# A GpSimd cast order, a per-head DMA transpose call and a planner rule in a fused attention and MLP kernel

## The chip, the cores and the metric

The kernel runs on one core of a Trainium2 chip. The metric is the device time of one execution in microseconds (us), the median of several runs. The engines named below are PE (TensorE, the matrix unit), DVE (VectorE), ACT (ScalarE), POOL (GpSimd) and SP (SyncE, which here only issues transfers). Each engine has its own instruction stream and works it off in order; 16 DMA engines move data for all of them.

## The reference

Eight batches, eight heads, 576 positions, head dimension 64. The first four heads ("plain") attend to the last 32 positions, the last four ("dilated") to every fourth of the last 128. The result, as 4608 rows of 512, goes through an MLP with 2048 hidden columns and a gated activation; its output is 4608 x 512 in float32.

```python
    window = 32
    dilation = 4
    scale = 1.0 / np.sqrt(D)
    scores = scale * np.matmul(q, k.transpose(0, 1, 3, 2))
...
    rel = pos[:, None] - pos[None, :]
    mask_plain = (rel >= 0) & (rel < window)
    mask_dil = (rel >= 0) & (rel < window * dilation) & (rel % dilation == 0)
...
    attn = attn / (np.sum(attn, axis=-1, keepdims=True) + 1e-09)
    return np.matmul(attn, v).astype(np.float32)
...
    h = x @ w_in
    g = h * (1.0 / (1.0 + np.exp(-beta * h)))
    return (g @ w_out).astype(np.float32)
```

## The kernel before

All inputs are float32, and the matmuls run in bfloat16. The 4608 token rows are cut into nine tiles of 512. Tile `t` needs the attention output `xT` of the batches that its rows lie in (a batch has 576 rows), then 16 groups of four matmuls with `w_in` (L887, one group for each 128 columns of the hidden layer), tanh on ACT (L896), the gate on DVE (L901), and four blocks of 16 matmuls with `w_out` (L922), whose sums ACT or DVE scale into one of four `osb` buffers (L937, L939) and SP stores (L942). The attention of batch `b` is worked in between the matmuls of tile `b - 1`.

The order on every engine is written down ahead of time. The program describes each step as an `Op` with the engines that may do it, a duration, dependencies and a due number `vt`; `Plan.run` (L64) plays the steps against its own model of engines, PSUM banks and DMA queues and emits them in the order that it finds. `NUDGE` (L47) shifts single steps by step number. Where PE would be idle in the model's first 80 us it emits a filler matmul on zeros (L1035).

Keys and queries reach PE with the head dimension on the partitions. For batches 0 to 2 they are loaded by position and turned on PE (L469, L479). For batches 3 to 7 (`b >= DIRECT`) each of four groups (`z` 0 keys, 1 queries; `h0` 4 the dilated heads, 0 the plain ones) takes two DMA steps:

- `cast` (L443): POOL issues a DMA from the float32 input to a bfloat16 scratch tensor in DRAM. Dilated groups are copied in the input's own order, as 16 x 9 runs of 1024 elements. Plain groups are copied into the order position, head, element, so in 2304 runs of 64 elements.
- `crossbar` (L453): SP issues one `dma_start_transpose` of the scratch tensor, viewed as 576 rows of 256 columns, into SBUF tiles of 128 partitions x 2 x 576: `dk` and `dq` for the dilated heads, `kT` and `qT` for the plain ones.

`loads(b)` (L985) starts them: POOL's one-element copy `pace` (L1001) waits until both halves of `xT` of batch `b - 2` and all four transposes of batch `b - 1` have landed; then come the casts, the value loads and, on SP, the transposes. The plain scores of a batch of this kind are 24 matmuls in one step, named `S00` (L711), which needs both `kT` and `qT`. The attention's result leaves through DRAM: SP stores `xsp`, `xdm` and `xdt` (L506, L514, L519) and turns them into `xT` (L533).

Of the kernel before, what the change touches and what calls it, by code (L numbers as in the profile page):

```python
# [39 lines left out]
class Plan:  # L40
# [3 lines left out]

    CAPS = {"h": 3, "p": 4, "o": 2, "z": 4, "a": 8, "s": 5, "w": 6}
    SWITCH = 95
    NUDGE = {9: -400, 35: 400, 78: -150, 90: 150, 103: -900, 156: -900, 164: -60, 191: -60, 208: 150,  # L47
        220: 900, 247: -400, 251: 60, 266: -150, 268: -150, 270: -150, 326: 900, 376: 400,
        397: 900, 420: 900, 432: -900, 490: 900, 525: 150, 545: 60, 554: 900, 562: -60, 571: 60,
        574: 150, 1103: -400, 1113: 400}  # L50
    LAT = {"PE": 210, "ACT": 45, "DVE": 45, "POOL": 60, "SP": 0}
    NEAR = {"PE": 40, "ACT": 60, "DVE": 60, "POOL": 60, "SP": 0}

# [10 lines left out]
    def run(self, filler=None, filler_until=0.0):  # L64
        free = {"PE": 1100.0, "ACT": 1300.0, "DVE": 1000.0, "POOL": 1300.0, "SP": 1300.0}
        dma_free = {"POOL": 0.0, "SP": 0.0, "ACT": 0.0}
        lanes = {"POOL": [], "SP": [], "ACT": []}
        bank_free = {b: 0.0 for b in self.banks}
        held = {}
        for o in self.ops:  # L70
            for d in o.deps:
                d.next.append(o)
            o.waits = len(o.deps)
            o.ready = 0.0
        avail = [o for o in self.ops if not o.waits]
        n_left = len(self.ops)
        n_held = {k: 0 for k in self.CAPS}
        ends = []
        halves = False
        port = {"DVE": 0.0, "POOL": 0.0}  # L80

        def release(now):
            for g in list(ends):
                if g.release <= now:
                    ends.remove(g)
                    n_held[g.kind] -= 1

        def bank_at(gs, start):
            kind, more = gs[0].kind, len(gs)
            n = [x.release for x in ends if x.kind == kind and x.release > start]  # L90
            n_open = sum(1 for x in held.values() if x.kind == kind)
            if n_open + more > self.CAPS[kind]:
                return None
            over = n_open + len(n) - self.CAPS[kind] + more
            if over > 0:
                start = sorted(n)[over - 1]
            open_banks = {x.bank for x in held.values()}
            times = sorted(t for b, t in bank_free.items() if b not in open_banks)
            return max(start, times[more - 1]) if len(times) >= more else None

        while n_left:
            best = None
            near = {}
            for o in avail:
                base = o.ready
                at = {e: max([free[e], base] + [t for x, t in o.group.read.items() if x != e]
                             if o.group is not None and e != "PE" else [free[e], base]) for e, d in o.engs}
                if o.sbuf:
                    at = {e: max(t, port["DVE" if e == "POOL" else "POOL"]) for e, t in at.items()}
                fin = min(at[e] + d for e, d in o.engs)  # L110
                for e, d in o.engs:
                    start = at[e]
                    if start + d > fin + 100:
                        continue
                    if o.dma and len(lanes[e]) >= 8:
                        start = max(start, lanes[e][-8])
                    if o.acquire is not None:
                        start = bank_at(o.acquire, start)
                        if start is None:
                            continue  # L120
                    near.setdefault(e, []).append((start, o, d))
            picks = []
            for e, c in near.items():
                first = min(s + o.bias for s, o, _ in c)
                s, o, d = min((x for x in c if x[0] + x[1].bias <= first + self.NEAR[e]), key=lambda x: (x[1].vt, x[0]))
                picks.append((s, o.vt, e, o, d))
            assert picks, "no work can start"
            s, _, e, o, d = min(picks, key=lambda x: (x[0], x[1]))
            if filler is not None and s <= filler_until and free["PE"] + (300 if free["PE"] < COLD else 170) < s:
                now = free["PE"]  # L130
                open_banks = {x.bank for x in held.values()}
                spare = [b for b, t in bank_free.items() if b not in open_banks and t <= now]
                if spare:
                    filler(max(spare, key=lambda b: -bank_free[b]))
                free["PE"] = now + (225 if now < COLD else 115)
                halves = False
                continue
            for g in o.acquire or ():
                open_banks = {x.bank for x in held.values()}
                g.bank = min((b for b, t in bank_free.items() if b not in open_banks and t <= s + 1e-6),  # L140
                             key=lambda b: -bank_free[b])
                held[id(g)] = g
                g.left = len(g.users)
            o.fn(e)
            if e == "PE" and o.halves != halves:
                halves = o.halves
                d += self.SWITCH
            free[e] = s + d
            if o.sbuf:
                port[e] = s + d  # L150
            o.start, o.end = s, s + d + self.LAT[e]
            if o.group is not None and e != "PE":
                o.group.read[e] = o.end
            if o.dma:
                at = max(dma_free[e], s + d + 900)
                other = max(dma_free.values()) - at
                dma_free[e] = at + o.dma + max(0.0, min(o.dma, other))
                o.end = dma_free[e] + (o.lat or 1100)
                lanes[e].append(o.end)
            avail.remove(o)  # L160
            n_left -= 1
            for x in o.next:
                x.waits -= 1
                x.ready = max(x.ready, o.end)
                if not x.waits:
                    avail.append(x)
            for g in list(held.values()):
                if o in g.users:
                    g.left -= 1
                    if not g.left:  # L170
                        del held[id(g)]
                        g.release = max(u.end for u in g.users)
                        bank_free[g.bank] = g.release
                        ends.append(g)
            ends[:] = [g for g in ends if g.release > s - 5000]
        self.end = max(free.values())
# [8 lines left out]
def kernel(  # L185
# [10 lines left out]
    nc = tc.nc  # L196
    P = 128
    B, H, S, D = q.shape
# [5 lines left out]
    WIN = 32  # L204
    C = 4
# [29 lines left out]
    plan = Plan(range(8))  # L235
# [47 lines left out]
    kT = [const([P, 2, WIN + S], BF16, f"kT{i}") for i in range(2)]  # L283
    qT = [const([P, 2, S], BF16, f"qT{i}") for i in range(2)]
    qt = [const([P, 2, 2, 4, UT], BF16, f"qt{i}") for i in range(2)]
    dk = [const([P, 2, 4, CT], BF16, f"dk{i}") for i in range(2)]
# [109 lines left out]
    def load(queue, args, deps, vt, kb, rate=.4, issue=750, lat=1100):  # L396
        return plan.op(
            [(queue, issue)],
            lambda e: dma(queue, *args), deps, vt, dma=kb * 1024 / rate / 1000, lat=lat)
# [41 lines left out]
    scratch = {}  # L441

    def cast(b, z, h0, deps, vt):  # L443

        dst = scratch[b, z, h0] = dram_pool.tile([S * 4 * D], BF16, name=f"s{b}_{z}_{h0}")
        src = (k, q)[z][b, h0:h0 + 4]
        if h0:
            args = [x.rearrange("(a c e) -> c a e", c=16, e=1024) for x in (dst[:], src.rearrange("h s d -> (h s d)"))]
        else:
            args = (dst[:].rearrange("(s h d) -> s h d", h=4, d=D), src.rearrange("h s d -> s h d"))  # L450
        return load("POOL", args, deps, vt, 576, .38 if h0 else .2, 500 if h0 else 1700)

    def crossbar(b, z, h0, deps, vt):  # L453
        kv = b % 2
        if h0:
            dst = (dk, dq)[z][kv][:].rearrange("p r h t -> p r (h t)")
        else:
            dst = qT[kv][:] if z else kT[kv][:, :, WIN:]
        src = scratch[b, z, h0][:].rearrange("(a e) -> a e", e=C * D)
        return plan.op([("SP", 1300)], lambda e: nc.sync.dma_start_transpose(out=dst, in_=src),  # L460
                       deps, vt, dma=288 * 1024 / .2 / 1000, lat=5500 if b == DIRECT else 6500)


# [605 lines left out]
```

## Time and profile before

| | us |
|---|---|
| median of 3 runs | 303.01 (302.78 to 303.18) |
| the profiled execution | 302.73 |
| its span in the trace | 301.0 |
| PE busy | 295.5 (98%) |
| DVE busy | 187.5 (62%) |
| ACT busy | 172.2 (57%) |
| POOL busy | 83.9 (28%) |
| plain transposes (L460): first `kT` issue, last `qT` issue | 67.0, 192.8 |
| plain scores `S00` of batches 3 to 7 (L711): first, last | 85.7, 215.2 to 215.7 |

The span runs from the first to the last instruction that the trace shows; the 1.7 us to the profiled execution's own time lie around it. An engine's busy time leaves out the issuing of DMAs, so SP has none; its instructions are listed as SPq, and their durations are those of the issue, not of the transfer.

### The profile page before, as it was taken

How to read it: one execution, taken by the hardware profiler on the slowest of the kernel's cores; microseconds unless marked ns; L12 is line 12 of the kernel's file. 1: busy time of each engine (PE TensorE's matmuls, PEld its weight loads, DVE VectorE, ACT ScalarE, POOL GpSimd, SP SyncE). 2: the span in 40 equal slices, each digit the busy share in tenths (PEclk: the TensorE clock that was granted, in tenths of full speed). 3: DMA queues.
4: the chain of work that ended last, by engine and by line, in shares of the span. 5: the costliest groups of instructions: out<-in, count | busy, mean ns of one | idle time of the engine just before them, and what ended most of it. 6: DMA issues, size and time to landing. Idle time of an engine off the chain costs nothing.

```text
span 301.0 us, 6071 instructions
## 1 busy us (share of the span) xinstructions
PE 295.5 (98%) x2344; PEld 150.4 (50%) x2344; DVE 187.5 (62%) x424; ACT 172.2 (57%) x311; POOL 83.9 (28%) x121
## 2 busy tenths in 40 slices
PE   8999999999999999999999999999999999999995
PEld 5866546444554445544444544444454444444454
DVE  4769787798857846887677647865772363343300
ACT  3868764867745744667484548454852654554311
POOL 8997324764236006400730074000000000000000
PEclk9999999999999999999999999999999999999999
DMA  8999999899889998999899979993124100100122
GB/s 164 188 210 201 206 178 222 122 133 145 196 188 197 158 199 173 199 158 191 145 172 158 224 146 173 179 211 90 37 74 117 70 1 35 37 35 35 59 82 70
DMA packets 111248, 41.98 MB, mean 139 GB/s; under 512 B 87620, under 2 KB 104596, under 8 KB 111220
## 3 DMA queue, kind: packets, MB, share of 16 engines
q0 software_dynamic: 60336, 18.58, 59.5%
q1 hardware_dynamic: 50740, 22.95, 37.8%
q8 instruction: 18, 0.29, 0.4%
q14 instruction: 10, 0.08, 0.1%
q10 hardware_dynamic: 144, 0.07, 0.1%
HBM read 37.76 MB, written 18.87 MB: 188 GB/s over the span
## 4 chain that ended last, share of the span: by engine, by line
PE 94%; DVE 2%; ACT 1%; POOL 1%; issue 1%; POOLq 0%; ACTq 0%
PE bank L922 41%; PE bank L887 40%; PE bank L804 2%; PE bank L1035 2%; PE bank L683 1%; PE bank L788 1%; PE bank L711 1%; PE bank L469 1%; PE bank L747 1%; PE bank L479 1%; ACT ptd L619 1%; PE bank L773 1%; DVE xdm L639 1%; PE bank L673 1%; DVE ptd L623 1%
## 5 line engine op out<-in xcount | busy, mean ns | idle before, releaser
L922 PE MATMUL bank<-w_out_bf,g 128*128 128x512 bf16 (+2 forms) x608 | 140.0, 368 | 0.0
L901 DVE SCALAR_TENSOR_TENSOR g<-tnh,bank 128x512 bf16<-128x512 bf16 x144 | 97.3, 685 | 68.2 <-ACT tnh L896 67.2
L896 ACT ACTIVATE tnh<-bank,beta_half 128x512 bf16<-128x512 f32 x144 | 97.9, 690 | 70.3 <-PE bank L887 63.8
L887 PE MATMUL bank<-xT,w_in_bf 128*128 128x512 bf16 (+1 forms) x584 | 137.0, 376 | 0.0
L887 PEld LDWEIGHTS <-w_in_bf 128*128 128x128 bf16 x584 | 55.7, 98 | 62.8 <-issue 0.3
L922 PEld LDWEIGHTS <-g 128*128 128x128 bf16 x608 | 54.5, 98 | 55.7
L937 ACT ACTIVATE osb<-bank 128x512 f32<-128x512 f32 (+1 forms) x35 | 20.6, 589 | 31.3 <-PE bank L922 30.7
L619 ACT ACTIVATE pt<-bank 128x384 bf16<-128x384 f32 (+1 forms) x54 | 20.8, 467 | 6.8 <-PE bank L711 4.3
L619 ACT ACTIVATE ptd<-bank 128x512 bf16<-128x512 f32 x32 | 16.8, 602 | 6.2 <-PE bank L683 6.2
L639 DVE TENSOR_TENSOR xsp<-bank,rcp 96x384 bf16<-96x384 f32 x32 | 17.7, 554 | 1.3 <-DVE rcp L638 0.2
L623 DVE TENSOR_TENSOR pt<-pt,mask_n 128x384 bf16<-128x384 bf16 (+1 forms) x41 | 14.8, 391 | 5.7 <-ACT pt L619 5.5
L638 DVE RECIPROCAL rcp<-bank 128x4 f32<-128x4 f32 (+2 forms) x72 | 12.8, 178 | 5.5 <-PE bank L804 2.4
L1001 POOL COPY pace<-xT 1x2 bf16<-1x2 bf16 x4 | 0.7, 175 | 51.2 <-DMA xT<-x 51.2
L394 POOL DMA_DIRECT2D vp<-in_v_dram x9 | 14.7, 1632 | 0.4 <-PE bank L469 0.4
L623 DVE TENSOR_TENSOR ptd<-ptd,mask_d 128x512 bf16<-128x512 bf16 x27 | 12.0, 465 | 3.6 <-ACT ptd L619 3.0
L639 DVE TENSOR_TENSOR xdm<-bank,rcp 128x256 bf16<-128x256 f32 x32 | 13.6, 425 | 1.1
L394 POOL DMA_DIRECT2D s<-in_q_dram x10 | 13.5, 1351 | 0.0
L394 POOL DMA_DIRECT2D vt<-in_v_dram x16 | 13.3, 993 | 0.0
L1035 PE MATMUL bank<-zero 128*128 128x256 bf16 x67 | 11.6, 310 | 1.3 <-DVE warm L302 1.1
L394 POOL DMA_DIRECT2D s<-in_k_dram x10 | 11.0, 1100 | 1.4 <-issue 1.1
L804 PEld LDWEIGHTS <-pt 128*128 128x128 bf16 x192 | 8.9, 97 | 4.7
L804 PE MATMUL bank<-vp,pt 128*128 128x65 bf16 x192 | 9.8, 193 | 0.0
(112 smaller groups left out, 172.2 us busy)
## 6 DMA issues: line engine op xcount, KB each, us to landing
out_dram<-osb SPq DMA_DIRECT2D x35, 256.0 KB
s<-in_k_dram POOLq DMA_DIRECT2D x10, 288.0 KB, 7.1
s<-in_q_dram POOLq DMA_DIRECT2D x10, 288.0 KB, 10.0
w_out_bf<-in_moe_w_out_dram POOLq DMA_DIRECT2D x2, 1024.0 KB, 16.5
vp<-in_v_dram POOLq DMA_DIRECT2D x7, 288.0 KB, 17.3
st<-in_q_dram POOLq DMA_DIRECT2D x6, 288.0 KB, 11.1
x<-xsp SPq DMA_DIRECT2D x12, 144.0 KB
st<-in_k_dram POOLq DMA_DIRECT2D x5, 288.0 KB, 13.2
```

The lines of the kernel that those rows point to most:

```text
L394: {"POOL": nc.gpsimd, "SP": nc.sync}[queue].dma_start(out=out, in_=in_)
L619: nc.scalar.activation(out=w(), in_=sc(), func=ACT.Exp, scale=SCALE)
L623: E[e].tensor_tensor(out=w(), in0=w(), in1=m(), op=ALU.mult)
L638: nc.vector.reciprocal(out=r, in_=p[..., D])
L639: nc.vector.tensor_tensor(out=dst, in0=p[..., 0:D], in1=r.unsqueeze(len(p.shape) - 1).to_broadcast(list(p.shape[:-1]) + [D]), op=ALU.mult)
L804: nc.tensor.matmul(pv[:, a, h2, :], lhsT=lhs, rhs=vp[kv][:, (2 * x + h2) * NI + 3 * j + a, 0:D + 1], start=True, stop=True)
L887: nc.tensor.matmul(bank(g)[:, a:z], lhsT=w_in_bf[:, kt, fb * P:(fb + 1) * P], rhs=xT[:, kt, xo + a:xo + z], start=(i == 0 and kt == kts[0] ...
L896: nc.scalar.activation(out=th[:, 0:n], in_=bank(g)[:, 0:n], func=ACT.Tanh, scale=beta_half[:, fb:fb + 1])
L901: nc.vector.scalar_tensor_tensor(out=g_t[t % 2][:, fb, c0:c0 + n], in0=th[:, 0:n], scalar=1.0, in1=bank(g)[:, 0:n], op0=ALU.add, op1=ALU.mult)
L922: nc.tensor.matmul(bank(g)[:, lo:hi], lhsT=g_t[t % 2][:, fb, tb * P:(tb + 1) * P], rhs=w_out_bf[:, fb, lo:hi], start=(fb == 0), stop=(fb = ...
L937: nc.scalar.mul(out=ob[:, lo:hi], in_=bank(g)[:, lo:hi], mul=0.5)
L1035: nc.tensor.matmul(BANKS[b][:, 0:256], lhsT=zero[:, 0:P], rhs=zero[:], start=True, stop=True)
```

## The change

Five edits:

- `cast`: the plain groups are copied in the input's own order too, in 16 x 9 runs of 1024 elements, with the planner's figures for a dilated group.
- `crossbar`: a plain group is brought in by four `dma_start_transpose` calls, one a head; each takes a 576 x 64 piece of the scratch tensor to 64 partitions x 576 of `kT` or `qT`. The planner counts 2400 ns of SP for them, in place of 1300. Dilated groups are as before.
- `Plan.run`: POOL steps marked `sbuf` are not planned to start before 1200 ns after the end of POOL's last DMA issue (`issued`).
- `NUDGE` has other entries.
- The order that the planner finds is another one.

```diff
+        issued = 0.0
...
+                if o.sbuf and "POOL" in at:
+                    at["POOL"] = max(at["POOL"], issued)
...
             if o.sbuf:
                 port[e] = s + d
+            elif o.dma and e == "POOL":
+                issued = s + d + 1200
...
-        if h0:
-            args = [x.rearrange("(a c e) -> c a e", c=16, e=1024) for x in (dst[:], src.rearrange("h s d -> (h s d)"))]
-        else:
-            args = (dst[:].rearrange("(s h d) -> s h d", h=4, d=D), src.rearrange("h s d -> s h d"))
-        return load("POOL", args, deps, vt, 576, .38 if h0 else .2, 500 if h0 else 1700)
+        args = [x.rearrange("(a c e) -> c a e", c=16, e=1024) for x in (dst[:], src.rearrange("h s d -> (h s d)"))]
+        return load("POOL", args, deps, vt, 576, .38, 500)
...
     def crossbar(b, z, h0, deps, vt):
         kv = b % 2
+        src = scratch[b, z, h0][:]
         if h0:
-            dst = (dk, dq)[z][kv][:].rearrange("p r h t -> p r (h t)")
+            parts = [((dk, dq)[z][kv][:].rearrange("p r h t -> p r (h t)"), src.rearrange("(a e) -> a e", e=C * D))]
         else:
-            dst = qT[kv][:] if z else kT[kv][:, :, WIN:]
-        src = scratch[b, z, h0][:].rearrange("(a e) -> a e", e=C * D)
-        return plan.op([("SP", 1300)], lambda e: nc.sync.dma_start_transpose(out=dst, in_=src),
+            parts = [((qT[kv][:, x] if z else kT[kv][:, x, WIN:])[D * h:D * h + D],
+                      src.rearrange("(n s d) -> n s d", n=4, d=D)[2 * x + h]) for x in range(2) for h in range(2)]
+
+        def turn(e):
+            for dst, part in parts:
+                nc.sync.dma_start_transpose(out=dst, in_=part)
+        return plan.op([("SP", 1300 if h0 else 2400)], turn,
                        deps, vt, dma=288 * 1024 / .2 / 1000, lat=5500 if b == DIRECT else 6500)
```

What the two programs hold for the plain keys of batch 3 on SP, as instructions in order (output, input, shape of the output):

```
before:  DmaTransposeAnt kT<-s   128x2x576      (source: 576 rows, step 256; 256 columns, step 1)
after:   DMACopy kT<-s   64x576x1   x4          (source: 64, step 1; 576, step 64; 1, step 1)
```

## The prediction

> **What bounds the kernel now.** I read the page's busy times, slices, queues and chain first, then SP's and POOL's timelines around batches 3 and 4, then PE's plain scores.
>
> ```profile
> span 301.0 us, 6071 instructions
> ...
> PE 295.5 (98%) x2344; PEld 150.4 (50%) x2344; DVE 187.5 (62%) x424; ACT 172.2 (57%) x311; POOL 83.9 (28%) x121
> ...
> PEclk9999999999999999999999999999999999999999
> DMA  8999999899889998999899979993124100100122
> ...
> q0 software_dynamic: 60336, 18.58, 59.5%
> q1 hardware_dynamic: 50740, 22.95, 37.8%
> ...
> PE 94%; DVE 2%; ACT 1%; POOL 1%; issue 1%; POOLq 0%; ACTq 0%
> ```
>
> PE is busy 98% of the span at full granted clock and holds 94% of the chain, so a transfer off that chain costs nothing while it lands in time. The 16 DMA engines, though, are near nine tenths busy until about 200 us: a transfer that needs more engine time has no idle ones to use.
>
> ```profile
> 59.91 2.17 SPq L460 DMA_TRANSPOSE dk<-s  x1
> 62.20 4.67 SPq L460 DMA_TRANSPOSE dq<-s  x1
> 66.96 3.89 SPq L460 DMA_TRANSPOSE kT<-s  x1
> ...
> 76.68 1.42 SPq L460 DMA_TRANSPOSE qT<-s  x1
> 78.20 1.03 SPq L506 DMA_DIRECT2D x<-xsp  x2
> 81.41 1.30 SPq L533 DMA_TRANSPOSE xT<-x  x1
> ...
> 98.82 2.93 SPq L460 DMA_TRANSPOSE kT<-s  x1
> ```
>
> SP's timeline (start, duration of the issue): the plain keys of batch 3 go out at 66.96, its queries at 76.68, the attention output of batch 2 behind them at 78.20, and the keys of batch 4 at 98.82. All are on one queue, in this order.
>
> ```profile
> 87.30 0.17 POOL L1001 COPY pace<-xT 1x2 bf16<-1x2 bf16 x1 [7.71 <-DMA xT<-x]
> 87.54 0.60 POOL L394 DMA_DIRECT2D s<-in_k_dram  x1
> 88.13 0.57 POOL L394 DMA_DIRECT2D s<-in_q_dram  x1
> 88.86 1.63 POOL L394 DMA_DIRECT2D s<-in_k_dram  x1 [0.16 <-issue]
> ```
>
> POOL starts batch 4's casts only when xT of batch 2 has landed (87.30).
>
> ```profile
> L711 PE MATMUL bank<-qT,kT x120: 202/203/214, 85.7 to 215.7; 64*128 64x96 bf16 x120
> ```
>
> The plain scores: five steps of 24 matmuls, from 85.7 us (batch 3) to 215.2 (batch 7, where PE's timeline has the fifth step begin). PE works in order, so everything behind S00 of a batch waits until that batch's kT and qT are there. The slack from qT's issue to S00 is 85.7 - 76.7 = 9.0 us in batch 3 and 215.2 - 192.8 = 22.4 in batch 7.
>
> **The change, part by part. First the crossbar.** The four calls of a plain group are not transposes in the built program: each has become an ordinary DMACopy whose source steps by one element over 64 columns and by 64 elements over 576 rows, with an inner run of one element. A group is then 4 x 64 x 576 = 147,456 two-byte elements where before it was 288 KB in 256-byte rows, 1,152 packets. If each element is a packet and 16 engines share them, one engine has 9,216 a group.
>
> No two-byte packet is in the trace of before, so I bound its price by the trace's packet records, grouped by queue and size. On SP's queue (q1) a packet of 4 bytes took 9 ns in the median and 12.9 in the mean (2,020 of them), 256 bytes 18 ns, 512 bytes 27, 2,048 bytes 86: a fixed part of about 9 ns and 9 ns for every 256 bytes. Below the fixed 9 ns a packet of its own should hardly go. The dearest small packet is POOL's 128-byte one (q0), 32 ns. The 4-byte packets are nearest in size, but they only count up a semaphore; the 256-byte ones are nearest in work, since they fetch from the same scratch and write to SBUF. I take halfway between 12.9 and 18, 15.45 ns, and keep 9 and 32 as ends. One group then takes T = 9,216 x 15.45 ns = 142.4 us (ends 82.9 and 294.9), against slack of 9 to 22 us.
>
> [...]
>
> Now the path. PE stands at S00 of batch b until qT(b) has landed, and the batches follow one another through pace: the casts of batch b + 1 wait for xT(b - 1), whose stores lie behind qT(b) on SP's queue. I walk it:
> - The keys of batch 3 still start at 67.0 us: SP has the same issues ahead of them, and the third cast's landing was not what they waited for (SP was issuing dq until 66.87).
> - Ten groups one after the other on one queue: 10 T = 1,424 us.
> - Four links from one qT landing to the next kT issue. Before: xsp store at 78.20 to xT issue at 81.41, 3.2; to pace at 87.30, 5.9; to kT of batch 4 at 98.82, 11.5; together 20.6, so 82.4.
> - The tail behind S00 of batch 7: 301.0 - 215.2 = 85.8. The new order leaves 472 matmuls behind that step, the old one 456; 16 x 0.216 us (four L922 matmuls take 0.86 in the chain) = 3.5 more, 89.3.
> - Fillers: 54 in place of 67, at 1.8% of 301.0 / 67 = 81 ns each on the chain, 1.05 us less ahead of the 67.0.
>
> 67.0 + 1,424 + 82.4 + 89.3 - 1.05 = 1,662 us of span; with the 1.7 around it (302.73 - 301.0) 1,663. By the same sum 9 ns gives 1,068, 12.9 gives 1,428, 18 gives 1,898, 32 gives 3,188. The profiled execution lies 0.3 us under the median of the runs, which is nothing here.
>
> What is queued behind these copies: on SP, the output stores (four osb buffers) and the xT transposes, and through them ACT's and DVE's L937 and L939 and PE. PE is waiting at S00 anyway, and four buffers carry one tile, about one batch's worth, so I add nothing; if PE stops short of S00 instead, at most a batch's spacing, (215.2 - 85.7) / 4 = 32.4 us, moves behind each of four landings, 130 us.
>
> **The casts.** A plain cast drops from 2,304 x 128 bytes to 1,024-element runs; 33 ns x 23,040 packets / 16 = 47.5 us of q0 time go over the run, and POOL's issue falls from 1.63 to about 0.6 us. It is worth nothing on the path: POOL waits 7.7 us ahead of pace, and PE doesn't wait for it. With that cover gone (the elements on the path), a faster cast shortens a link by at most the (1.63 - 0.60) us of issue and some of its landing, under 8 us x 4.
>
> **The POOL rule and the nudges.** Masks and copies trade places between POOL, DVE and ACT: ptd and ptt on POOL go from one each to two, dkt from 3 to 5, vp from 2 to 1. Those engines are at 28 to 62%, so off the path; cover gone, a POOL mask of 2.4 us (ptd at 61.51) where DVE takes 0.47 delays one value step by 2 us. Bounds: minus 1.05 (fillers) to plus 2 x 3.
>
> **The rivals.**
> 1. The elements cost little. If the engine merges the contiguous write run of 576 elements, or the copy costs only its bytes (294,912 / 16 at 256 bytes per 9 ns = 0.65 us), T hides and the kernel is as the planner meant it: 303.01 - 1.05 = 302.0 us, faster. The place is S00; it decides where 2T + 20.6 fits the 32.4 us between two S00, so at T of 5.9 us, 0.64 ns an element and engine. For it: the destination rows are contiguous. Against: the source isn't, and 0.64 ns is a fourteenth of the cheapest packet seen.
> 2. Reads alone pay, and half of the 9 ns: T = 41.5, 239 + 415 = 654 us. [...] Against: nothing in the trace splits it.
> 3. SP's issue is the bound. dk's issue took 2.17 us for 1,152 packets, a store of 128 rows about 0.46: 1.71 / 1,024 = 1.7 ns a packet. 147,456 of them are 246 us a group, 239 + 2,460 = 2,700. For it: SP's transposes take 1.4 to 4.7 us to issue. Against: a plain copy of 288 rows (x<-xsp) issues in 0.5 us, no longer than the 128-row store.
>
> **How the numbers follow.** The forecast's case, packets of 9 to 32 ns one by one on the engines: 0.80. Rival 1: 0.03, with another 0.01 for a time within 0.2% of before, which is about what a measurement of this kernel can tell from no change. Rival 2: 0.08. Rival 3: 0.08. The time is that of the forecast, 1,663. The range goes from 1,050 (just under the 9 ns sum) to 2,900 (28.9 ns by the same sum); it leaves out rivals 1 and 2 and the dearest packets, and holds rival 3. Slower: 0.80 + 0.08 + 0.08 = 0.96; faster 0.03; same 0.01.
>
> **What would show it.** SP's rows for kT and qT as plain DMA copies, x4 a group; about 1.47 million more packets on q1, with a mean of 9 to 32 ns; PE idle ahead of L711 in each of the five batches by up to 2T, released by the transfer of qT; pace 20 us apart from the last element of the batch before; L711's last step some 89 us ahead of the end. The prediction is wrong if q1's packet count stays near 50,000, if PE's long waits are anywhere other than L711 (osb's, or dkt's on POOL), or if SP's own issues are long and the engines idle beside them.

## The result, and the profile after

| | before | after |
|---|---|---|
| median, us | 303.1 (302.78 to 303.6, 4 runs) | 2148.22 (2131.69 to 2160.93, 4 runs) |
| span of the profiled execution, us | 301.0 | 2159.2 |

The changed kernel takes 7.09 times as long (95% interval 7.066 to 7.106). The forecast was 1,663 us in a range of 1,050 to 2,900. The page of the changed kernel:

```profile
PE 314.6 (15%) x2331; PEld 155.4 (7%) x2331; DVE 186.6 (9%) x421; ACT 173.2 (8%) x309; POOL 77.4 (4%) x126
...
PEclk9855555575555555755555575555555755555589
DMA  9999999999999999999999999999999999999931
GB/s 190 54 2 2 12 2 2 2 88 1 2 2 4 2 2 51 35 1 1 2 2 2 2 83 1 2 2 2 2 2 58 32 2 2 2 2 2 2 78 49
...
q1 hardware_dynamic: 1514100, 22.96, 162.8%
q0 software_dynamic: 38736, 18.58, 6.8%
...
SPq 84%; PE 9%; DMA 4%; another core or an unknown queue 1%; DVE 1%; POOL 1%; issue 0%; ACT 0%; POOLq 0%
```

PE's two longest waits on the same page:

```profile
L896 PE MATMUL bank<-xT,w_in_bf 128*128 128x512 bf16 (+1 forms) x584 | 145.4, 391 | 1110.0 <-DMA xT<-x 1108.4
L720 PE MATMUL bank<-qT,kT 64*128 64x96 bf16 x120 | 5.6, 230 | 722.7 <-DMA qT<-s 722.7
```

PE's work is as before but for some 19 us, and now fills 15% of the span. The DMA engines are busy nine tenths or more in all slices but the last two, yet in most of them they move 1 to 4 GB/s. SP's queue (q1) has 1,514,100 packets in place of 50,740, with 22.96 MB in place of 22.95. The chain that ended last has changed hands from PE to SP's issues. SP's timeline around batches 3 and 4 (start, duration):

```profile
65.21 4.40 SPq L468 DMA_TRANSPOSE dq<-s  x1
69.71 145.47 SPq L468 DMA_DIRECT2D kT<-s  x4
215.27 46.12 SPq L951 DMA_DIRECT2D out_dram<-osb  x1
...
264.15 134.76 SPq L468 DMA_DIRECT2D qT<-s  x4
399.01 45.68 SPq L951 DMA_DIRECT2D out_dram<-osb  x1
444.79 0.91 SPq L515 DMA_DIRECT2D x<-xsp  x2
449.75 3.35 SPq L542 DMA_TRANSPOSE xT<-x  x2
...
470.35 147.88 SPq L468 DMA_DIRECT2D kT<-s  x4
```

The plain keys are four plain copies, and an output store behind them takes SP 46 us to issue, where the longest of such stores took 0.58 us in the kernel before. PE's timeline shows whom it waits for, in batch 3 and ahead of batch 7:

```profile
313.90 0.26 PE L720 MATMUL bank<-qT,kT 64*128 64x96 bf16 x1 [226.78 <-DMA qT<-s]
359.50 0.66 PE L720 MATMUL bank<-qT,kT 64*128 64x96 bf16 x11 [45.34 <-DMA qT<-s]
405.11 0.24 PE L720 MATMUL bank<-qT,kT 64*128 64x96 bf16 x1 [44.96 <-DMA qT<-s]
449.41 0.64 PE L720 MATMUL bank<-qT,kT 64*128 64x96 bf16 x11 [44.06 <-DMA qT<-s]
```

```profile
2060.33 8.67 PE L896 MATMUL bank<-xT,w_in_bf 128*128 128x512 bf16 x28 [366.75 <-DMA xT<-x]
2068.83 1.03 PE L931 MATMUL bank<-w_out_bf,g 128*128 128x512 bf16 x4
2069.79 0.69 PE L720 MATMUL bank<-qT,kT 64*128 64x96 bf16 x24
```

In batch 3 (and 4) PE stands at the plain scores and gets on as the four copies of the queries land, one after the other. From batch 5 it stands earlier, at the matmuls of a tile that need xT of the batch before, whose store and transpose lie behind the elements on SP's queue.

POOL's timeline has pace for batch 4 (`pace` holds back the casts of the next batch), which stood 372 us for xT of batch 2, where before it was 7.7:

```profile
455.43 0.17 POOL L1010 COPY pace<-xT 1x2 bf16<-1x2 bf16 x1 [372.08 <-DMA xT<-x]
```

The trace's packet records, one for each packet of a transfer, give the price. The 294,912 two-byte elements of a batch take 371.6, 375.7, 378.0, 377.2 and 371.1 us from the first to the last, 374.7 in the mean: with 18,432 for each of 16 engines, 20.3 ns an element. Below, "ns an element" is always this time of one engine.

### The profile page after: what moved, and what is told of

The parts are those of the page before. It is cut to its first block, busy times and chain, and to the rows that moved or that the text cites. A ratio compares the mean times of both kernels' runs of the same rounds, so it can differ in the third digit from the quotient of the medians.

```text
span 2159.2 us, 6092 instructions
## 1 busy us (share of the span) xinstructions
PE 314.6 (15%) x2331; PEld 155.4 (7%) x2331; DVE 186.6 (9%) x421; ACT 173.2 (8%) x309; POOL 77.4 (4%) x126
## 3 DMA queue, kind: packets, MB, share of 16 engines
q1 hardware_dynamic: 1514100, 22.96, 162.8%
q0 software_dynamic: 38736, 18.58, 6.8%
## 4 chain that ended last, share of the span: by engine, by line
SPq 84%; PE 9%; DMA 4%; another core or an unknown queue 1%; DVE 1%; POOL 1%; issue 0%; ACT 0%; POOLq 0%
SPq L468 69%; SPq L515 11%; PE bank L931 4%; SPq L951 4%; PE bank L896 4%; DMA dq<-s 1%; DMA vp<-in_v_dram 1%; DMA xT<-x 1%; DMA st<-in_k_dram 1%; DMA s<-in_k_dram 0%; DMA x<-xsp 0%; PE bank L692 0%; DVE g L910 0%; PE bank L797 0%
## 5 line engine op out<-in xcount | busy, mean ns | idle before, releaser
L896 PE MATMUL bank<-xT,w_in_bf 128*128 128x512 bf16 (+1 forms) x584 | 145.4, 391 | 1110.0 <-DMA xT<-x 1108.4
L931 PE MATMUL bank<-w_out_bf,g 128*128 128x512 bf16 (+2 forms) x608 | 148.2, 382 | 0.0
L896 PEld LDWEIGHTS <-w_in_bf 128*128 128x128 bf16 x584 | 56.9, 101 | 1178.9 <-DMA xT<-x 736.7
L720 PE MATMUL bank<-qT,kT 64*128 64x96 bf16 x120 | 5.6, 230 | 722.7 <-DMA qT<-s 722.7
L720 PEld LDWEIGHTS <-kT 64*128 64x128 bf16 x120 | 3.8, 107 | 725.9 <-issue 453.1
L647 DVE RECIPROCAL rcp<-bank 128x4 f32<-128x4 f32 (+2 forms) x72 | 12.9, 179 | 14.0 <-PE bank L813 8.0
L401 POOL DMA_DIRECT2D vp<-in_v_dram x9 | 10.2, 1133 | 0.1
```

The source lines that it names most:

```text
L401: {"POOL": nc.gpsimd, "SP": nc.sync}[queue].dma_start(out=out, in_=in_)
L896: nc.tensor.matmul(bank(g)[:, a:z], lhsT=w_in_bf[:, kt, fb * P:(fb + 1) * P], rhs=xT[:, kt, xo + a:xo + z], start=(i == 0 and kt == kts[0] ...
L931: nc.tensor.matmul(bank(g)[:, lo:hi], lhsT=g_t[t % 2][:, fb, tb * P:(tb + 1) * P], rhs=w_out_bf[:, fb, lo:hi], start=(fb == 0), stop=(fb = ...
```

## The experiments

Two questions were open: whether the elements alone make the loss, and what sets their 20.3 ns. The first nine runs have the order of the changed kernel, and each of them was run once. "Keys only" is the ground for the other eight: queries come in as before, so five groups of elements are left instead of ten. The price is in each case the time from a group's first to its last element in the packet records, mean of the five groups, over the elements of one engine. The expectations weigh two theories: by A each element costs its DMA engine 20.3 ns, by B SP's queue makes them at a fixed 1.27 ns each, whatever the engines do; W, R and Q come later.

**Keys only**

```diff
+        elif z:
+            parts = [(qT[kv][:], src.rearrange("(a e) -> a e", e=C * D))]
         else:
-            parts = [((qT[kv][:, x] if z else kT[kv][:, x, WIN:])[D * h:D * h + D], ...
+            parts = [(kT[kv][:, x, WIN:][D * h:D * h + D], src.rearrange("(n s d) -> n s d", n=4, d=D)[2 * x + h])
+                     for x in range(2) for h in range(2)]
```

> Only the keys of batches 3 to 7 are brought in by elements; the queries have their position-major cast and whole-group crossbar transpose back. Five groups of 147,456 elements in place of ten. Theory A (each element is a packet that costs its DMA engine about 20.3 ns: 374 us for two groups of 9,216 packets an engine) and theory B (SP's queue makes descriptors at 1.27 ns an element, whatever the engines do) both take 5 x 187 us off the span of 2,159: about 1,225 us. If the time came from the new order, the nudges or the clock and not from the elements, it would stay well above 1,500.

Measured: 1,233.65 us, span 1,232.0; a group 188.5 us, 20.4 ns an element. Half the elements take half the loss with them: 2,159.2 - 1,232.0 = 927 us for five groups.

**Two queues**

```diff
-            for dst, part in parts:
-                nc.sync.dma_start_transpose(out=dst, in_=part)
+            for n, (dst, part) in enumerate(parts):
+                q = nc.scalar if len(parts) == 4 and n % 2 else nc.sync
+                q.dma_start_transpose(out=dst, in_=part)
```

> As the keys-only run, but two of the four element copies of a group are issued from ACT, on its own queue. Theory A (the 16 engines are the bound): no change, about 1,225 us. Theory B (one queue's descriptor making is the bound): the two queues work side by side, a group takes 94 us, about 755 us.

Measured: 850.07 us, a group 114.8 us, 12.5 ns. The engines can do better than 20.3 ns, so theory A falls as it was put. Over the whole group theory B's halving isn't quite met; through the middle of a group it is (35 us of the first: an element every 10.0 ns, against some 20 in the keys-only run), and the rest is the change from one copy to the next and the end. But this run is confounded: the copies on ACT's queue are those to partitions 64 to 127, SP's those to 0 to 63.

**Four bytes**

```diff
+            parts = [(kT[kv][:, x, WIN:][D * h:D * h + D].bitcast(FP32),
+                      src.rearrange("(n e) -> n e", n=4)[2 * x + h].bitcast(FP32).rearrange("(s d) -> s d", d=D))
...
+                    nc.sync.dma_start(out=dst.unsqueeze(2), in_=part.rearrange("s d -> d s").unsqueeze(2))
```

> As the keys-only run, but the same bytes are moved as four-byte elements, 288 a row in place of 576, so half the packets; pairs of neighbouring head elements stay together, so the plain keys of batches 3 to 7 are permuted and their scores are other numbers. If a packet costs the same at 2 and at 4 bytes, a group takes 94 us and the kernel about 755 us. If the bytes or their read and write cost it (half the rate for whatever reason in a 2-byte write only), other values: 1,225 if it goes by bytes.

Measured: 507.46 us, a group 44.0 us (counted over the dense run of element packets, since q1 has other four-byte packets too, 2,020 in the kernel before, read as those that count up semaphores). The span says the same: 1,232.0 - 505.8 = 726 us less, 145 a group, leaves 43 of the 188.5. SP's view of this line:

```profile
L475 SPq DMA_DIRECT2D kT<-s x20: 647/10667/15921, 67.2 to 379.3; - x20
```

The same bytes in half the packets take less than a quarter of the time: 9.5 ns a packet where two bytes took 20.4. So it doesn't go by bytes, and a packet has no one price either: a four-byte one is cheaper. Why that is wasn't settled.

**Eight engines**

```diff
+            parts = [(kT[kv][:, x, WIN:][D * h + 8 * r:D * h + 8 * r + 8],
+                      src.rearrange("(n s d) -> n s d", n=4, d=D)[2 * x + h][:, 8 * r:8 * r + 8])
+                     for x in range(2) for h in range(2) for r in range(8)]
```

> As the keys-only run, but each copy is cut into eight of 8 partitions, 32 a group with 4,608 elements each, so that the outermost size is 8. If such a copy is spread over 8 engines and the engines are the bound (theory A), a group takes twice 187 us and the kernel about 2,160 us. If the queue's descriptor making is the bound (theory B), or the copy is spread over 16 engines after all, about 1,225 us; the number of 4-byte packets a copy (8 or 16) says which.

Measured: 3,592.86 us, a group 659.6 us, 3.5 times 188.5, outside both theories. The 140 copies more have 960 four-byte packets more on q1 (3,140 against 2,180), which is what 160 copies at 8 and 20 at 16 give (ACT's one store in the changed kernel, 128 rows, has 144 packets on q10, so 16 beside its rows); read as one such packet an engine, each copy used 8 engines, and an element cost its engine 35.8 ns. SP's view of this line:

```profile
L474 SPq DMA_DIRECT2D kT<-s x160: 709/20418/25031, 67.3 to 3435.8; - x160
```

A copy of 4,608 elements took SP 20.4 us in the median to issue, 4.4 ns an element, against 45.7 us for 36,864 in the keys-only run, 1.2 ns. In the changed kernel itself the shortest issue of 36,864 elements was 0.65 us:

```profile
L468 SPq DMA_DIRECT2D kT<-s x20: 649/46377/55502, 69.7 to 1776.4; - x20
```

The issue is therefore no fixed price an element. That a long issue follows the transfers ahead of it on the queue is how these rows are read; what SP waits for in it isn't shown.

**Writes apart**

```diff
+            flat = kT[kv][:].rearrange("p x s -> p (x s)")
+            parts = [(flat[D * h:D * h + D, WIN + x:WIN + x + 2 * S - 1:2], src.rearrange("(n s d) -> n s d", n=4, d=D)[2 * x + h])
```

> As the keys-only run (1,232 us of span, 20.2 ns an element and engine), but an engine's neighbouring two-byte writes lie four bytes apart: the element copies of a group write every second element over both halves of the key tile, so the plain keys of batches 3 to 7 lie in other places and their scores are other numbers. Theory W (a two-byte write has to wait for the one before it in the same word): the price falls to that of the four-byte run, 12 to 14 ns, a group takes about 120 us and the span is about 900 us. Theory Q (one queue keeps a fixed number of packets open, whatever they write): no change, about 1,232 us.

Measured: 1,223.66 us, 20.3 ns. Neighbouring writes in one word are not it. (The 12 to 14 ns that the expectation gives the four-byte run is too high, it was 9.5; with 20.3 measured, theory W falls either way.)

**A farther source** (the cast's condition, then the copies)

```diff
-        if h0 or not z:
+        if h0:
...
+            parts = [(kT[kv][:, x, WIN:][D * h:D * h + D], src.rearrange("(s n d) -> n s d", n=4, d=D)[2 * x + h])
```

> As the keys-only run, but the keys are cast position-major as in the kernel before, so that neighbouring elements lie 512 bytes apart in the source in place of 128; the writes are the same. If the reads set the price (four-byte elements lay 256 bytes apart and were cheaper), it moves: by theory R (nearer reads collide) to 14 ns or less, span about 950 us or less; if far reads are dearer, above 1,250. Theories W and Q: no change, 1,232 us, but for the slower cast of the keys, under 10 us.

Measured: 1,248.58 us, 20.8 ns. The distance between the positions that are read one after the other is not it either.

**Sixteen neighbours, and sixteen spread** (the first two lines, and the last two)

```diff
+            parts = [(kT[kv][:, x, WIN:][D * h + 16 * r:D * h + 16 * r + 16],
+                      src.rearrange("(n s d) -> n s d", n=4, d=D)[2 * x + h][:, 16 * r:16 * r + 16])
...
+            parts = [(kT[kv][:, x, WIN:][D * h + r:D * h + D:4],
+                      src.rearrange("(n s d) -> n s d", n=4, d=D)[2 * x + h][:, r::4])
```

> As the keys-only run, but each copy is cut into four of 16 partitions, 16 a group with 9,216 elements each: a control for the run with 8 partitions, which took 36 ns an element and engine. With 16 engines at work again and one partition each, 20 ns and about 1,235 us are expected if the number of engines is what counted there; if it is that the partitions of one copy lie close together, a group takes more than 187 us, up to twice, and the span goes towards 2,160 us.

> As the keys-only run, each copy cut into four of 16 partitions like the run with 16 neighbouring partitions (38.5 ns an element and engine, 2,074 us), with the same sizes and number of copies, but the 16 partitions of a copy are every fourth of the 64. [...] If it is one partition an engine, or the many short copies, that made that run slow: 38 ns again, about 2,070 us.

Measured: 2,075.45 us and 38.6 ns for neighbours; 1,298.97 us and 21.8 ns for the spread. Both have 80 copies of 9,216 elements, counted over 16 engines; what differs is which 16 partitions a copy writes to, and with them which 16 columns of the scratch it reads. In the spread run the single groups took 184 to 223 us, so its 21.8 is no sure step above 20.4. One partition an engine and the many short copies, which both runs have, are therefore not what made the first slow; what counts is how close together the partitions, and source columns, of a copy lie, 38.6 ns against 21.8. Whether that is in writing or in reading isn't parted: a partition and a source column go together in every run here, and the farther source only moved the positions apart.

**Both halves**

```diff
+            parts = [(kT[kv][:, x, WIN:], src.rearrange("(s x p) -> x p s", x=2, p=P)[x].unsqueeze(2)) for x in range(2)]
```

> The keys are cast position-major, as in the kernel before, and come in by two element copies a group over all 128 partitions, in place of four over 64, on SP's one queue; number and size of the elements are the same as in the keys-only run. [...] Theory Q (one queue keeps a fixed number of packets open): 20 ns, span about 1,240 us.

Measured: 893.82 us, a group 120.3 us, 13.0 ns, on one queue. The keys-only price of 20 ns is gone without a second queue, so theory Q falls. The q1 lines of this run, then of the keys-only run:

```profile
q1 hardware_dynamic: 782260, 22.95, 136.4%
```

```profile
q1 hardware_dynamic: 782420, 22.95, 149.1%
```

The same bytes in as many packets but for 160 (ten copies less, at 16 four-byte packets); the price goes with how many partitions, and source columns, a copy covers: 13.0 ns over 128, 20.4 over 64.

**The rest of the change, twice.** First the old casts and crossbars under the changed kernel's order, then with their own planner figures too, so that the order is planned for them.

```diff
+            parts = [(qT[kv][:] if z else kT[kv][:, :, WIN:], src.rearrange("(a e) -> a e", e=C * D))]
```

> The plain casts and the whole-group crossbar transposes of the kernel before are put back, with the order, the nudges and the POOL rule of the changed kernel. If all the loss is in the element copies and the rest is off the path, 302.0 us: 13 fillers of 81 ns less than before. Bounds of the prediction's working: 301.9 to 309. Had the new order a loss of its own, it would show here as more than 303.5.

Measured: 306.59 us, ratio 1.0124 (1.0104 to 1.0144). Not the 302.0 expected. PE's waits, which the kernel before doesn't have:

```profile
140.45 0.62 PE L694 MATMUL bank<-dq,dk 64*128 64x128 bf16 x16 [1.24 <-DVE g L912]
171.07 0.60 PE L694 MATMUL bank<-dq,dk 64*128 64x128 bf16 x15 [1.53 <-DVE g L912]
```

The second run has `cast` and `crossbar` word for word from the kernel before, with the POOL rule and the nudges of the changed one.

> The two transfer edits undone with their planner figures, so that the order is planned for what is issued; the POOL rule and the nudges of the changed kernel stay, 55 fillers in place of 67. The run with the old transfers in the new order was 1.24% slower than before (306.6 us) with PE waits of 1.2 to 1.5 us ahead of dilated scores, which the kernel before does not have. If that came from an order planned for casts and transposes of other lengths, this run is at 302 to 304 us and those waits are gone; if the POOL rule or the nudges cost it, it stays at 305 to 308.

Measured: 311.44 us, ratio 1.0297 (1.0259 to 1.0334), slower still. The waits ahead of the dilated scores are gone, but another one has come:

```profile
129.20 0.59 PE L894 MATMUL bank<-xT,w_in_bf 128*128 128x512 bf16 x1 [4.87 <-DMA xT<-x]
```

The granted clock is 0.89 in the stretch from 120 to 150 us around it, where before it was 1.00. So 12 or 13 fillers less bring no gain in either order. Whether the POOL rule or the nudges cost the 3 to 8 us was not tried apart. One row goes the rule's way: POOL's mask on `ptd`, 2.42 us in the kernel before, takes 1.15 and 1.17 us in the changed one; that the rule is the cause is not shown.

**The calls as they read**: a crossbar transpose a head that stays one, with 128 columns.

```diff
+            wide = lambda n, h: bass.AP(tensor=src.tensor, offset=src.offset + n * S * D - D * h, ap=[[D, S], [1, 2 * D]])
+            parts = [(((qT, qT2) if z else (kT, kT2))[h][kv][:, x, 0 if z else WIN:], wide(2 * x + h, h))
+                     for x in range(2) for h in range(2)]
```

> The change as its calls read, with a crossbar transpose a head that stays one: each takes 576 rows of 128 columns, 64 of them the head's and 64 of the next or the last position's, which land in the unused half of the partitions; the second head of a pair has tiles of its own. Casts in the input's order as in the changed kernel. If such transposes cost like the whole-group ones, 18 ns for 256 bytes, two for one, they hide (2.6 us a group) and the time is that of the run with the rest alone, 302.0 within 0.5 us. If SP's issue of four transposes a group (1.4 to 4.7 us each) makes kT or qT late at the first plain scores, where there were 9 us, it is some us above 303.

Measured: 326.85 us, ratio 1.080 (1.0758 to 1.0842): slower, as the second of the two had it, but by 24 us and at another place than the one named, since PE waits for xT and nowhere for kT or qT. SP's timeline of batches 3 and 4:

```profile
67.85 7.66 SPq L472 DMA_TRANSPOSE kT<-s  x4
...
88.24 2.70 SPq L546 DMA_TRANSPOSE xT<-x  x2
...
107.90 7.58 SPq L472 DMA_TRANSPOSE kT<-s  x4
```

Four calls take 7.7 us to issue where one took 3.9, and xT of batch 2 goes out at 88.2 in place of 81.4. From batch 3's keys to batch 7's it is 210.5 - 67.9 = 142.6 us, before 188.1 - 67.0 = 121.1: 21.5 us of the 24 or so lost lie in this round of pace, casts and transposes. Before, PE had no wait for xT; here it waits 11.4 us in all for it, so the round is read as what sets the pace. In this order, and with the quicker casts in hand, the change still loses.

## Why the prediction was right, point by point

**The mechanism** of the loss was as told: the four calls a group are element copies, on the path, and 1,463,360 packets more on q1 (1,474,560 elements and 320 packets of 4 bytes, less the 11,520 of 256 bytes that they replace). Keys only shows that the loss goes with their number, and the run with the old transfers (306.6 us) that hardly any is left without them. Where PE stands was told only in part. Its long waits are at the plain scores in batches 3 and 4 alone; the page puts 722.7 us there (L720) and 1,108.4 at L896, for xT. So one of the prediction's own signs of being wrong came up, long waits elsewhere than at the plain scores. It had priced that case, with up to 130 us, and it cost 14.7, in the tail below. Rival 1 (merged or hidden elements) and rival 2 (4.5 ns) are out by 20.3 ns; rival 2's half of a packet's price for the reads was a supposition that no run shows. Rival 3 (SP's issue at 1.7 ns a packet) is out as a mechanism: an element's share of the issue was 4.4 ns, 1.2 and, for the shortest, 0.02 (0.65 us for 36,864).

**The sum**, term by term, in us of the profiled span:

| term | predicted | measured |
|---|---|---|
| start of batch 3's keys | 66.0 | 69.7 |
| ten groups, 10 T | 1,424 | 1,873.7 |
| issue to first element, five times | in no term | 28.8 |
| four links from qT's last element to the next kT issue | 82.4 | 83.1 |
| last element to the end | 89.3 | 104.0 |
| sum | 1,662 | 2,159.3 |

Elements are placed by the packet records, whose clock runs 9.0 us ahead of the page's (their last packet set at the span's end). That setting is an assumption: each microsecond that it is off moves 5 us between the third row and the two below it (4 and 1), and leaves the sum as it is. The term that was mis-sized is T: 15.45 ns an element predicted, 20.3 measured, 450 of the 497 us. Three things were wrong in taking it from records. The two that it halved aren't alike: 12.9 ns is the mean of the 4-byte records and 18 the median of the 256-byte ones, whose mean in the same trace is 30.2; halfway between the medians is 13.5, between the means 21.6. A record is no price: here the two-byte records last 39 ns in the median and 37.1 in the mean, above the 9 to 32 that were foretold, and one comes every 20.3, so two are open at a time, and q1's share of the engines adds up to 162.8%. And the price isn't the packet's alone, as the experiments show: 13 to 39 ns by the partitions that a copy covers. That 20.3 lies between the ends of 9 and 32 ns is therefore in part luck: the sum had no term for the place, and 16 neighbouring partitions would have been outside.

The links come out within 1 us by this placing, so the 20.6 us of pace, casts and transposes held about as read from the kernel before. The tail missed a step: PE was expected at the plain scores, and in batches 5 to 7 it stood ahead of them, at L896, for xT of the batch before. So after the last element come the xT transpose (landed 5.1 us later), 28 matmuls at a granted clock of 0.73, and only then S00 at 2,069.8; from there to the end it is 89.4, as predicted.

**The casts** were rightly at nothing: q0 has 38,736 packets in place of 60,336 and 6.8% of a span seven times as long. The links, where a faster cast could have gained, are no shorter for it.

**The POOL rule and the nudges** had bounds of minus 1 to plus 6 us, with 1.05 us of gain taken. The two runs of the rest are 3.4 and 8.5 us slower, the second beyond the bound, in an order planned anew. The gain by fillers was wrong as a step: it counted the PE work saved ahead of batch 3 and left out what another order costs behind it.

## What to carry to other kernels

Look at the built program, not at the call: a transpose call with 64 columns had become a copy with one packet an element, and that line alone told the sign and the order of size. Price many small packets by the time from the first to the last of a run of them, not by a record's length (20.3 ns against 39 here), and ask how close together the partitions written and the columns read by one copy lie: 13.0 ns over 128, 38.6 over 16 neighbours. Ahead of an edit of a hidden transfer, measure the whole round that releases the next one: a real crossbar a head, a few us longer on SP, cost 24 us although PE nowhere waited for kT or qT.

## What the runs showed of the hardware

Two-byte elements, counted over 16 engines, cost an engine 13.0 ns each where the copy covers 128 partitions, 20.3 to 21.8 over 64 neighbours or every fourth of them, and 38.6 over 16 neighbours; counted over 8 engines, 35.8 over 8 neighbours; four-byte ones over 64 neighbours cost 9.5. In the changed kernel and with both halves the two-byte records lasted twice their spacing (39 ns against 20.3, 26 against 13.0), so two were open at a time in each.

Why the price goes with the place is not shown. No run parts the writes from the reads: the four-byte run's 64 columns span 256 bytes, as the 128 columns of both halves do, and these two are the cheapest on one queue (9.5 and 13.0 ns). The two-queue run, whose queues wrote to different halves, had an element every 10.0 ns through the middle of a group, so the 13.0 of both halves on one queue is no floor of an engine; what sets it isn't shown either.

While PE waited, its granted clock was 0.50 (from 90 to 450 us), and 0.73 in the first 10 us after the last wait; 1.00 again from 2,070 us on.
